# Attention, MLP and experts on one core: the decay of the keys as two rows of the score product

## Chip, core and metric

One core of a Trainium2 chip. The metric is the device time of the program in microseconds (us), the median of several runs; lower is better. In the profile, PE is the tensor engine's matmuls and PEld its weight loads, DVE is VectorE, ACT is ScalarE, POOL is GpSimd, and SP is the engine whose queue issues all the DMAs of this kernel.

## The reference

```python
def _attn_ref(q, k, v, s):                       # B, H, S, D = 2, 8, 576, 64
    scores = scale * np.matmul(q, k.transpose(0, 1, 3, 2))
    causal = np.triu(np.ones((S, S), dtype=bool), k=1)
    cum = np.cumsum(np.maximum(s, 0.0), axis=-1)
    bias = -(cum[:, :, :, None] - cum[:, :, None, :])
    scores = np.where(causal, -1000000000.0, scores + np.minimum(bias, 0.0))
    scores = scores - np.max(scores, axis=-1, keepdims=True)
    attn = np.exp(scores)
    attn = attn / (np.sum(attn, axis=-1, keepdims=True) + 1e-09)
    return np.matmul(attn, v)

x = attention output as (1152 tokens, 512)
h = x @ w_in;  x = np.maximum(0.01 * h, h) @ w_out                # 512 -> 2048 -> 512
out = sum over 4 experts e of p[:, e] * (np.maximum(x @ w1[e], 0) @ w2[e])   # 512 -> 1024 -> 512
```

Below the diagonal the bias is the key's decay sum less the query's. The query's part is the same for a whole row of the softmax and falls out, so the kernels add only the decay sum of the key.

## The kernel before

**Numbers.** Many matmuls use each operand as a pair of fp32r tiles: a high part (a cast on ACT) and the rest (a subtraction on POOL or DVE). The weights of the first MLP are 64-bit values in DRAM. `convert` (L91 to L106) makes fp32 of them, 16 pieces in all: two DMAs of 512 KB at L99 into one of two buffers `r64` (named r in the trace), one pass on ACT (L102) and four on DVE (L103 to L106). The piece is written back for later use (L115), and split by ACT (L140) and POOL (L141).

**Attention.** It is cut into 16 units of one batch, one pair of heads and a range of query tiles of 128: first 8 early units (tiles 0 and 1, keys 0 to 255), then 8 late ones (tiles 2 to 4, all 576 keys). `attention` runs the (tile, head) items of the units in a row, each in four steps with a lag between them: `scores`, `transposes`, `values`, `finish`. `load_pair` issues the loads of a unit when the unit before it begins (of the first two at the start).
- `cumulative` makes the decay sums of the 16 heads (L386), and writes them to DRAM (`cum_d`, L390).
- `load_pair` loads keys (`kr`, two heads on 128 partitions) and queries, and the tile `nck`: the decay sums of the unit's two heads on all 128 partitions, by a DMA that reads the same two rows 128 times (L446). Only the first unit gets it from four small matmuls and two copies on ACT (L442, L443). In early units the queries go to zero-padded tiles `qz` (L436), and the product is one fp32 matmul (L477). In late units queries and keys are split, `qs` (L425, L426) and `ks` (L430, L431), and the product is two matmuls (L480).
- `scores` writes the mask with an `affine_select` on POOL into 128 columns of `nck` (L473), once for each of the 80 items. Then the matmul, and on DVE L481, which adds `nck` to the scores, scales them into `z` and takes the row's minimum into `mn`. ACT does the exponential (L485).

**Order.** The early units run alone at first (with the first weights fetched after the second). The late units are woven into the first MLP's products over the first 512 tokens (`weave`, RATE = 5 attention steps to one of the MLP's); what is left of the attention runs by itself, then the rest. The order of instructions on each engine is set when the kernel is built, by a scheduler that simulates the program, within the data's order. All DMAs go through SP's queue in that order, and since their eight semaphores take turns, at most eight are on their way.

In the quoted order of SP's queue below, `r_...` are pieces of 64-bit weights, `vs` values, `w_f` the write-back.

## Time and profile before

| | us |
|---|---|
| median of 3 runs | 747.65 (745.64 to 748.36) |
| the profiled execution, its own time | 745.97 |
| its span in the trace | 744.2 |
| PE busy | 714.9 (96%) |
| DVE busy | 441.6 (59%) |
| POOL busy | 360.0 (48%) |
| ACT busy | 330.0 (44%) |

The three runs differ by 2.7 us. The span is divided as follows, by the first scores, the end of the early units and the end of the attention: to 62 us the early units with the first weights, to 185 us the late units among the first MLP's products with the conversion of the weights, to 221 us the rest of the attention, and then the remaining MLP and the experts. Times in the rows are microseconds unless marked ns. "Idle before" is the idle time of an engine just ahead of the instructions of a row, and behind it stand what ended it.

### The profile page before, as it was taken

How to read it: one execution, taken by the hardware profiler on the slowest of the kernel's cores; microseconds unless marked ns; L12 is line 12 of the kernel's file. 1: busy time of each engine (PE TensorE's matmuls, PEld its weight loads, DVE VectorE, ACT ScalarE, POOL GpSimd, SP SyncE). 2: the span in 40 equal slices, each digit the busy share in tenths (PEclk: the TensorE clock that was granted, in tenths of full speed). 3: DMA queues.
4: the chain of work that ended last, by engine and by line, in shares of the span. 5: the costliest groups of instructions: out<-in, count | busy, mean ns of one | idle time of the engine just before them, and what ended most of it. 6: DMA issues, size and time to landing. Idle time of an engine off the chain costs nothing.

```text
span 744.2 us, 11570 instructions
## 1 busy us (share of the span) xinstructions
PE 714.9 (96%) x4284; PEld 647.6 (87%) x4284; DVE 441.6 (59%) x919; ACT 330.0 (44%) x723; POOL 360.0 (48%) x326
## 2 busy tenths in 40 slices
PE   8888979997999989999999999999999999999997
PEld 7677868886988889999998988989889898898996
DVE  4788989959549472773674443644435444454452
ACT  5776957667765365563351232322313223142220
POOL 3487736556318658885436270542705427053200
PEclk9888999998999999999999999999999999999999
DMA  6997685854001222321011110201102011020002
GB/s 165 245 329 256 226 264 199 252 196 148 33 2 57 67 77 95 105 85 57 30 57 57 56 58 1 86 29 57 57 0 86 29 58 57 1 76 10 1 29 99
DMA packets 42792, 70.56 MB, mean 95 GB/s; under 512 B 4432, under 2 KB 25168, under 8 KB 42736
## 3 DMA queue, kind: packets, MB, share of 16 engines
q1 hardware_dynamic: 42736, 69.84, 29.3%
q8 instruction: 33, 0.54, 0.3%
q14 instruction: 23, 0.19, 0.1%
HBM read 59.04 MB, written 10.78 MB: 94 GB/s over the span
## 4 chain that ended last, share of the span: by engine, by line
PE 84%; DVE 7%; DMA 3%; issue 2%; ACT 2%; SPq 1%; POOL 1%; POOLq 0%; DVEq 0%; ACTq 0%
PE ps_d L188 38%; PE ps_u L188 34%; PE ps_o L503 5%; PE ps_sc L480 3%; PE ps_pt L494 3%; DMA nck<-cum_d 2%; DVE raw L105 1%; DVE z L481 1%; DVE raw L106 1%; PE ps_sc L477 1%; SPq L81 1%; DVE st L505 1%; DVE raw L103 1%; PE nothing L379 1%; DVE raw L104 0%
## 5 line engine op out<-in xcount | busy, mean ns | idle before, releaser
L188 PE MATMUL ps_u<-t,w 128*128 128x320 f32 (+1 forms) x1680 | 236.9, 299 | 2.4 <-DVE y L226 1.6
L188 PEld LDWEIGHTS ps_u<-t,w 128*128 128x128 f32 x1680 | 233.0, 189 | 6.3 <-DVE y L226 1.9
L188 PE MATMUL ps_d<-w,ht 128*128 128x512 f32 x864 | 202.9, 390 | 0.0
L188 PEld LDWEIGHTS ps_d<-w,ht 128*128 128x128 f32 x864 | 160.1, 188 | 31.7
L141 POOL TENSOR_TENSOR w<-raw,w 128x1024 fp32r<-128x1024 f32 x40 | 99.2, 2491 | 150.0 <-ACT w L140 149.8
L284 ACT ACTIVATE ht<-ps_u 128x320 fp32r<-128x320 f32 (+1 forms) x128 | 50.6, 411 | 131.9 <-DVE ps_u L261 114.2
L300 DVE SCALAR_TENSOR_TENSOR oacc<-ps_d,pn,oacc 128x512 f32<-128x512 f32 x63 | 47.3, 750 | 104.0 <-PE ps_d L188 104.0
L188 PE MATMUL ps_d<-ht,w 128*128 128x320 f32 (+1 forms) x576 | 107.2, 341 | 0.3 <-issue 0.3
L188 PEld LDWEIGHTS ps_d<-ht,w 128*128 128x128 f32 x576 | 92.9, 190 | 8.3 <-issue 0.5
L133 POOL TENSOR_TENSOR w<-raw,w 128x512 fp32r<-128x512 f32 (+1 forms) x48 | 49.5, 1053 | 75.8 <-ACT w L132 75.8
L140 ACT CAST w<-raw 128x1024 fp32r<-128x1024 f32 x40 | 41.7, 1050 | 81.4 <-PE ps_d L188 70.2
L473 POOL TENSOR_SCALAR_AFFINE_SELECT nck<-nck 128x128 f32<-128x128 f32 x80 | 38.0, 487 | 73.8 <-DVE mn L481 40.7
L503 PEld LDWEIGHTS ps_o<-vs,pv 128*128 128x128 f32 x480 | 67.2, 206 | 6.0 <-DVE xo L509 3.2
L261 DVE TENSOR_TENSOR ps_u<-ps_u,tmp 128x320 f32<-128x320 f32 (+1 forms) x120 | 55.9, 470 | 25.5 <-PE ps_u L188 23.6
L503 PE MATMUL ps_o<-vs,pv 128*128 128x64 f32 x480 | 68.8, 282 | 1.9 <-DVE xo L509 1.8
L285 DVE SCALAR_TENSOR_TENSOR ht<-ps_u,ht 128x320 fp32r<-128x320 f32 (+1 forms) x128 | 56.3, 452 | 22.7 <-ACT ht L284 21.3
L261 DVE TENSOR_TENSOR tmp<-ps_u,tmp 128x320 f32<-128x320 f32 (+1 forms) x80 | 36.8, 463 | 43.3 <-PE ps_u L188 41.4
L133 POOL TENSOR_TENSOR w<-sums,w 128x1024 fp32r<-128x1024 f32 x24 | 58.2, 2427 | 7.8 <-ACT w L132 7.8
L485 ACT ACTIVATE z<-z,mn 128x256 f32<-128x256 f32 (+4 forms) x80 | 48.5, 607 | 20.8 <-DVE mn L481 18.5
L481 DVE CUSTOM_DVE_ANT_0 z<-ps_sc,nck 128x256 f32<-128x256 f32 (+4 forms) x80 | 40.6, 511 | 21.2 <-POOL nck L473 8.6
L188 PE MATMUL ps_u<-x,w 128*128 128x512 f32 x192 | 50.6, 408 | 0.5 <-ACT x L527 0.5
L480 PE MATMUL ps_sc<-ks,qs 128*128 128x128 f32 (+3 forms) x128 | 37.9, 386 | 11.5 <-DVE mn L481 9.4
(82 smaller groups left out, 779.9 us busy)
## 6 DMA issues: line engine op xcount, KB each, us to landing
raw<-in_moe_w_dram SPq DMA_DIRECT2D x32, 512.0 KB, 3.5
r<-in_moe_w_in_dram SPq DMA_DIRECT2D x16, 512.0 KB, 5.6
w_f<-raw SPq DMA_DIRECT2D x16, 512.0 KB, 3.3
r<-in_moe_w_out_dram SPq DMA_DIRECT2D x16, 512.0 KB, 5.6
raw<-w_f SPq DMA_DIRECT2D x16, 512.0 KB, 3.2
nck<-cum_d SPq DMA_DIRECT2D x8, 576.0 KB, 4.7
qr<-in_q_dram SPq DMA_DIRECT2D x16, 160.0 KB, 4.9
kr<-in_k_dram SPq DMA_DIRECT2D x8, 288.0 KB, 5.7
```

The source lines that it names most:

```text
L133: nc.gpsimd.tensor_tensor(lo, of, f32(hi), ALU.subtract)
L140: nc.scalar.copy(w[:, 0], raw)
L141: nc.gpsimd.tensor_tensor(w[:, 1], raw, f32(w[:, 0]), ALU.subtract)
L188: nc.tensor.matmul(ps, a, b, start=(i == 0 and not onto), stop=(i == len(pairs) - 1), skip_group_check=onto)
L261: nc.vector.tensor_tensor(to, of, x, ALU.add)
L284: nc.scalar.activation(hi, of, AF.Relu)
L285: nc.vector.scalar_tensor_tensor(lo, of, 0.0, f32(hi), ALU.max, ALU.subtract)
L300: nc.vector.scalar_tensor_tensor(oacc[tt], ps, p, oacc[tt], ALU.mult, ALU.add)
L480: nc.tensor.matmul(ps, self.qz[:, l, j, own], self.kr[:, j, keys], start=(l == 0), stop=(l == 1))
L481: nc.vector.tensor_tensor_reduce(out=z[:, keys], in0=ps, in1=nck[:, j, keys], scale=-(D ** -0.5), scalar=3.0e38 if pc == 0 else mn[:, 0:1] ...
L485: nc.scalar.activation(z, z, AF.Exp, bias=mn[:, pc : pc + 1], scale=-1.0, accum_out=self.st[i][:, j : j + 1])
L503: nc.tensor.matmul(o[:, j], pv[:, kt], self.vs[:, kt, j], start=(kt == 0), stop=(kt == i))
```

## The change

The mask becomes one fixed tile `mask` (made once: a memset and one affine_select), of which DVE adds a slice. The decay sums are rounded to fp32r and a rest (`cum2`), and these two rows are partitions 64 and 65 of the key tile, loaded by two small DMAs per unit (L442: from SBUF for the first unit, from `cum_d` for the others). The query tiles hold ones in these rows. An early product then runs over 66 rows (D + 2). The keys of an early unit stand in a tile `ke` of three buffers, the two heads side by side on 64 partitions. In a late unit `ks` has the high part of the keys on partitions 0 to 63 and the rest on 64 to 127; a second tile `kd` has a copy of the high part, made by a DMA from SBUF to SBUF (L439), and the two decay rows. The tile `kr` has one buffer instead of two.

```diff
-    cum_d = dram.tile([BH, S], F32, name="cum_d")
+    cum_d = dram.tile([2, BH, S], F32, name="cum_d")
+    mask = ap.tile([P, S], F32, name="mask", bufs=1)
...
-        cum0 = r64p.tile([P, 2048], F32R, tag="r64", name="cum0")[:BH, : 2 * half[0]].rearrange("p (l k) -> p l k", l=2)
-        nc.scalar.copy(cum0[:, 0], cum[:, : half[0]])
-        nc.vector.tensor_tensor(cum0[:, 1], cum[:, : half[0]], f32(cum0[:, 0]), ALU.subtract)
-        nc.sync.dma_start(cum_d, cum)
+        cum2 = r64p.tile([P, 2048], F32R, tag="r64", name="cum2")[:BH, : 2 * S].rearrange("p (l k) -> p l k", l=2)
+        nc.scalar.copy(cum2[:, 0], cum)
+        nc.vector.tensor_tensor(cum2[:, 1], cum, f32(cum2[:, 0]), ALU.subtract)
+        nc.sync.dma_start(cum_d.rearrange("l h k -> h l k"), f32(cum2))
+        nc.gpsimd.memset(mask, 0.0)
+        nc.gpsimd.affine_select(mask[:, S - P :], mask[:, S - P :], [[-1, P]], ALU.is_ge, MASKED, 0, 1)
...
     def load_pair(n, b, hp, i0, i1):
...
-        kr = ap.tile([P, S], F32, tag="kr", name="kr")
-        nc.sync.dma_start(kr[:, :q1], k[b].rearrange("h d s -> (h d) s")[rows, :q1])
...
+        if i0 == 0:
+            kd = early.tile([P, 2, half[0]], F32, tag="ke", name="ke", bufs=3)
+            nc.sync.dma_start(kd[:D], k_of)
+            qs = q_e[n % 3]
+            nc.sync.dma_start(qs[:D], q[b, heads, :, q0:q1].rearrange("h d s -> d h s"))
+            ks = None
+        else:
...
             for j in range(2):
-                own, other = slice(j * D, (j + 1) * D), slice((1 - j) * D, (2 - j) * D)
-                nc.scalar.copy(ks[own, j], kr[own])
-                nc.gpsimd.tensor_tensor(ks[other, j], kr[own], f32(ks[own, j]), ALU.subtract)
-            kr = ks
-        else:
-            qz = q_pads[n % 2]
-            for j in range(2):
-                nc.sync.dma_start(qz[j * D : (j + 1) * D, j, : q1 - q0], q[b, 2 * hp + j, :, q0:q1])
-        nck = ap.tile([P, 2, S], F32, tag="nck", name="nck")
-        if n == 0:
-...
-        else:
-            src = cum_d[h : h + 2, 0:q1]
-            nc.sync.dma_start(nck[:, :, :q1], bass.AP(tensor=src.tensor, offset=src.offset, ap=[[0, P], [S, 2], [1, q1]]))
+                nc.sync.dma_start(qr[j * D : (j + 1) * D], q[b, heads, :, q0:q1].rearrange("h d s -> d h s"))
+            qs = q_s[n % 2]
+            nc.scalar.copy(qs[:, 0], qr)
+            nc.gpsimd.tensor_tensor(qs[:D, 1], qr[:D], f32(qs[:D, 0]), ALU.subtract)
+            kr = ap.tile([P, 2, S], F32, tag="kr", name="kr", bufs=1)[:D]
+            nc.sync.dma_start(kr, k_of)
+            ks = ap.tile([P, 2, S], F32R, tag="ks", name="ks")
+            nc.scalar.copy(ks[:D], kr)
+            nc.gpsimd.tensor_tensor(ks[D:], kr, f32(ks[:D]), ALU.subtract)
+            kd = ap.tile([P, 2, S], F32R, tag="kd", name="kd")
+            nc.sync.dma_start(f32(kd[:D]), f32(ks[:D]))
+        for l in range(2):
+            decay = f32(cum2[h : h + 2, l, :q1]) if n == 0 else cum_d[l, h : h + 2, :q1]
+            nc.sync.dma_start(f32(kd[D + l : D + l + 1]), decay)
...
         def scores(self, i, j):
...
-            nc.gpsimd.affine_select(nck[:, j, a:kw], nck[:, j, a:kw], [[-1, P]], ALU.is_ge, MASKED, 0, 1)
...
-                if len(self.qz.shape) == 3:
-                    nc.tensor.matmul(ps, self.qz[:, j, own], self.kr[:, keys], start=True, stop=True)
+                if self.ks is None:
+                    nc.tensor.matmul(ps, self.qs[:DK, j, own], self.kd[:DK, j, keys], start=True, stop=True)
                 else:
-                    for l in range(2):
-                        nc.tensor.matmul(ps, self.qz[:, l, j, own], self.kr[:, j, keys], start=(l == 0), stop=(l == 1))
+                    nc.tensor.matmul(ps, self.qs[:, 0, j, own], self.ks[:, j, keys], start=True, stop=False)
+                    nc.tensor.matmul(ps, self.qs[:DK, 1, j, own], self.kd[:DK, j, keys], start=False, stop=True)
                 nc.vector.tensor_tensor_reduce(
-                    out=z[:, keys], in0=ps, in1=nck[:, j, keys], scale=-(D ** -0.5),
+                    out=z[:, keys], in0=ps, in1=mask[:, S - kw + keys.start : S - kw + keys.stop], scale=-(D ** -0.5),
```

What the scheduler makes of it, at three places. POOL, from its instructions for the third early unit to the first piece of weights (L141 is the low part of a piece; behind each instruction stand the semaphores it waits for), before:

```order
L473 AFFINE_SELECT nck<-nck 128x128 [waits DMAHW0_49,Pool_49]
L473 AFFINE_SELECT nck<-nck 128x128
L473 AFFINE_SELECT nck<-nck 128x128 [waits DVE_49] x2
L473 AFFINE_SELECT nck<-nck 128x128 [waits DMAHW5_49,Pool_49]
L473 AFFINE_SELECT nck<-nck 128x128
L473 AFFINE_SELECT nck<-nck 128x128 [waits DVE_49] x2
L473 AFFINE_SELECT nck<-nck 128x128 [waits DMAHW3_49,Pool_49]
L473 AFFINE_SELECT nck<-nck 128x128
L473 AFFINE_SELECT nck<-nck 128x128 [waits DVE_49] x2
L473 AFFINE_SELECT nck<-nck 128x128 [waits DMAHW2_49,Pool_49]
L473 AFFINE_SELECT nck<-nck 128x128
L473 AFFINE_SELECT nck<-nck 128x128 [waits DVE_49]
```

and after, from the last of the memsets to the second late unit's queries:

```order
L410 MEMSET qe_142 2x512
L410 MEMSET qe_144 2x512
L410 MEMSET qe_146 2x512
L392 AFFINE_SELECT mask<-mask 128x128 [waits Pool_49]
L432 TENSOR_TENSOR qs<-qr,qs 64x640 [waits DMAHW2_49,Activation_49]
L437 TENSOR_TENSOR ks<-kr,ks 64x1152 [waits DMAHW1_49,Activation_49,Pool_49]
L141 TENSOR_TENSOR w<-raw,w 128x1024 [waits Activation_49,Pool_49]
L141 TENSOR_TENSOR w<-raw,w 128x1024 [waits Activation_49]
L432 TENSOR_TENSOR qs<-qr,qs 64x640 [waits DMAHW4_49,Activation_49]
```

The affine_selects between the pieces are gone; nothing of the early units is left on POOL, and its first work after the start is the first late unit's split and the weights. SP's queue from the third unit's decay sums to the fifth unit's and the next weights, before:

```order
L446 DMA nck<-cum_d 128x2x256 [waits DMAHW0_49,DVE_49,Activation_49]
L99 DMA r_395<-in_moe_w_in_dram 128x2x512 [waits DMAHW1_49]
L436 DMA qz_138<-in_q_dram 64x256 [waits DMAHW2_49,PE_49]
L417 DMA kr<-in_k_dram 128x256 [waits DMAHW3_49,PE_49]
L436 DMA qz_138<-in_q_dram 64x256 [waits DMAHW4_49]
L446 DMA nck<-cum_d 128x2x256 [waits DMAHW5_49,DVE_49]
L448 DMA vs<-in_v_dram 128x2x128 [waits DMAHW6_49,PE_49]
L436 DMA qz_135<-in_q_dram 64x256 [waits DMAHW7_49,PE_49]
L417 DMA kr<-in_k_dram 128x256 [waits DMAHW0_49,PE_49]
L436 DMA qz_135<-in_q_dram 64x256 [waits DMAHW1_49]
L99 DMA r_395<-in_moe_w_in_dram 128x2x512 [waits DMAHW2_49]
L446 DMA nck<-cum_d 128x2x256 [waits DMAHW3_49,DVE_49]
L99 DMA r_405<-in_moe_w_in_dram 128x2x512 [waits DMAHW4_49]
L99 DMA r_405<-in_moe_w_in_dram 128x2x512 [waits DMAHW5_49]
```

and after, from the fourth unit's keys on:

```order
L422 DMA ke<-in_k_dram 64x2x256 [waits DMAHW2_49,PE_49]
L424 DMA qe_142<-in_q_dram 64x2x256 [waits DMAHW3_49]
L442 DMA ke<-cum_d 1x2x256 [waits DMAHW4_49]
L442 DMA ke<-cum_d 1x2x256 [waits DMAHW5_49]
L99 DMA r_353<-in_moe_w_in_dram 128x2x512 [waits DMAHW6_49]
L99 DMA r_353<-in_moe_w_in_dram 128x2x512 [waits DMAHW7_49]
L99 DMA r_363<-in_moe_w_in_dram 128x2x512 [waits DMAHW0_49]
L99 DMA r_363<-in_moe_w_in_dram 128x2x512 [waits DMAHW1_49]
L429 DMA qr<-in_q_dram 64x2x320 [waits DMAHW2_49]
L422 DMA ke<-in_k_dram 64x2x256 [waits DMAHW3_49,PE_49]
```

The first four weight loads stand in a row, behind the fourth unit's loads and ahead of the fifth's. Before, one half of the first piece stood ahead of the fourth unit's loads, the other among the fifth's, and the second piece behind these. SP's queue around the loads of a late unit in the middle of the attention, before:

```order
L446 DMA nck<-cum_d 128x1152 [waits DMAHW5_49,DVE_49]
L115 DMA w_f_73<-raw 128x1024 [waits DMAHW6_49,DVE_49]
L450 DMA vs<-in_v_dram 64x128 [waits DMAHW7_49,PE_49]
L423 DMA qr<-in_q_dram 64x2x320 [waits DMAHW0_49,Pool_49]
L423 DMA qr<-in_q_dram 64x2x320 [waits DMAHW1_49]
L99 DMA r_1551<-in_moe_w_in_dram 128x2x512 [waits DMAHW2_49]
L99 DMA r_1551<-in_moe_w_in_dram 128x2x512 [waits DMAHW3_49]
L417 DMA kr<-in_k_dram 128x576 [waits DMAHW4_49,Pool_49]
```

and after:

```order
L442 DMA kd<-cum_d 1x1152 [waits DMAHW7_49,PE_49]
L442 DMA kd<-cum_d 1x1152 [waits DMAHW0_49]
L446 DMA vs<-in_v_dram 64x128 [waits DMAHW1_49,PE_49]
L439 DMA kd<-ks 64x1152 [waits DMAHW2_49,Activation_49]
L429 DMA qr<-in_q_dram 64x2x320 [waits DMAHW3_49,Pool_49]
L429 DMA qr<-in_q_dram 64x2x320 [waits DMAHW4_49]
L115 DMA w_f_73<-raw 128x1024 [waits DMAHW5_49,DVE_49]
L99 DMA r_1883<-in_moe_w_out_dram 128x1024 [waits DMAHW6_49]
L434 DMA kr<-in_k_dram 64x2x576 [waits DMAHW7_49,Pool_49]
L99 DMA r_1883<-in_moe_w_out_dram 128x1024 [waits DMAHW0_49]
```

Where the broadcast load stood are two one-row loads, and the copy kd<-ks, which waits for ACT, stands ahead of the next unit's qr, the write-back and the next weight piece.

## Rows read from the trace of the kernel before

**Rows 1.** Windows: us, busy us (instructions) by engine, clock, DMA share, GB/s
```profile
0.00:62.00 62.00, 50.65 (x262) 42.23 (x262) 44.88 (x143) 39.28 (x120) 33.60 (x56) 0.85 0.86 257
62.00:185.00 123.00, 113.24 (x667) 98.75 (x666) 107.48 (x194) 87.96 (x174) 76.91 (x61) 0.94 0.66 215
185.00:221.00 36.00, 34.98 (x288) 32.88 (x287) 17.36 (x70) 26.06 (x65) 8.10 (x16) 1.00 0.06 19
221.00:744.00 523.00, 516.03 (x3073) 473.75 (x3073) 271.91 (x514) 176.69 (x365) 241.37 (x194) 1.00 0.16 53
```

**Rows 2.** The same view for 8 to 62 us
```profile
8.00:62.00 54.00, 44.47 (x238) 37.37 (x238) 41.65 (x138) 36.76 (x115) 30.45 (x41) 0.83 0.93 281
```

**Rows 3.** Chain of waits in 0 to 62 us, shares by line
```profile
by line: DMA nck<-cum_d 25.6%; PE ps_sc L477 9.4%; PE ps_o L503 9.1%; issue 7.3%; PE nothing L379 6.1%; DVE z L481 5.7%; DVE raw L105 4.8%; PE ps_pt L494 4.6%; DVE raw L103 4.1%; DVE raw L106 3.7%; POOL nck L473 3.4%; DVE st L505 2.7%; PE p
```

**Rows 4.** Waits, 0 to 62 us: line waited for, us, times, longest
```profile
POOL nck L473 <- DMA nck<-cum_d: 13.7, 6, 3.8
DVE z L481 <- POOL nck L473: 8.6, 6, 2.5
ACT qs L425 <- DMA qr<-in_q_dram: 2.0, 1, 2.0
```

**Rows 5.** Waits of PE in 62 to 185 us
```profile
PE ps_sc L480 <- DVE mn L481: 9.4, 4, 4.8
```

**Rows 6.** Groups to 222 us: busy us, mean ns | idle before, releasers
```profile
L106 DVE SCALAR_TENSOR_TENSOR raw<-r,raw 128x1024 uint32<-128x1024 uint32 x16 | 27.1, 1694 | 0.0
L505 DVE TENSOR_SCALAR st<-st 128x2 f32<-128x2 f32 x40 | 20.3, 507 | 5.5 <-ACT z L485 5.1
L473 POOL TENSOR_SCALAR_AFFINE_SELECT nck<-nck 128x128 f32<-128x128 f32 x80 | 38.0, 487 | 73.8 <-DVE mn L481 40.7 <-DMA nck<-cum_d 25.4 <-ACT nck L443 4.1
L141 POOL TENSOR_TENSOR w<-raw,w 128x1024 fp32r<-128x1024 f32 x14 | 36.5, 2607 | 3.3 <-ACT w L140 3.0
L431 POOL TENSOR_TENSOR ks<-kr,ks 64x576 fp32r<-64x576 f32 x16 | 24.7, 1545 | 3.5 <-issue 2.3
L426 POOL TENSOR_TENSOR qs<-qr,qs 128x640 fp32r<-128x640 f32 x8 | 17.5, 2190 | 11.5 <-ACT qs L425 11.5
```

**Rows 7.** Lines: shortest/median/longest ns, first, last start (L106: 62 to 185 us)
```profile
L505 DVE TENSOR_SCALAR st<-st x40: 150/169/2367, 9.6 to 214.5; 128x2 f32<-128x2 f32 x40
L473 POOL TENSOR_SCALAR_AFFINE_SELECT nck<-nck x80: 288/295/1298, 7.5 to 211.2; 128x128 f32<-128x128 f32 x80
L106 DVE SCALAR_TENSOR_TENSOR raw<-r,raw x13: 1211/1225/3067, 61.0 to 179.7; 128x1024 uint32<-128x1024 uint32 x13
```

**Rows 8.** Timeline at 171.8 us: start, duration
```profile
171.75 2.39 POOL L141 TENSOR_TENSOR w<-raw,w 128x1024 fp32r<-128x1024 f32 x1 [0.89 <-ACT w L140]
171.86 2.31 DVE L505 TENSOR_SCALAR st<-st 128x2 f32<-128x2 f32 x1
```

**Rows 9.** Timeline, VectorE's first score step
```profile
7.87 0.42 DVE L481 CUSTOM_DVE_ANT_0 z<-ps_sc,nck 128x256 f32<-128x256 f32 x1 [2.38 <-POOL nck L473]
```

**Rows 10.** DMA issues to 222 us: KB each, median us from issue to landing
```profile
nck<-cum_d SPq DMA_DIRECT2D x8, 576.0 KB, 4.7
kr<-in_k_dram SPq DMA_DIRECT2D x8, 288.0 KB, 5.7
qr<-in_q_dram SPq DMA_DIRECT2D x16, 160.0 KB, 4.9
r<-in_moe_w_in_dram SPq DMA_DIRECT2D x16, 512.0 KB, 5.6
cum_d<-cum SPq DMA_DIRECT2D x1, 36.0 KB, 1.6
```

**Rows 11.** Timeline, the last unit's key cast and first score product
```profile
192.05 0.67 ACT L430 CAST ks<-kr 64x576 fp32r<-64x576 f32 x1
202.41 0.45 PE L480 MATMUL ps_sc<-ks,qs 128*128 128x448 f32 x1
```

**Rows 12.** Waits of the DMA queue to 222 us
```profile
SPq L446 <- DVE mn L481: 21.2, 7, 8.3
```

More of the change, by code (lines that the diff above doesn't have):

```diff
@@ L367, in attention_moe_moe2 @@
     BH = B * H
-    cum_d = dram.tile([BH, S], F32, name="cum_d")
-    cum0 = None
-    pick = const.tile([BH, 2], F32R, name="pick")
+    cum_d = dram.tile([2, BH, S], F32, name="cum_d")
+    cum2 = None
+    mask = ap.tile([P, S], F32, name="mask", bufs=1)
     def cumulative():
-        nonlocal cum0
+        nonlocal cum2
         idle = ap.tile([P, P], F32, tag="idle", name="idle", bufs=1)
@@ L380, in cumulative @@
         pos, cum = (r64p.tile([P, 2048], F32, tag="r64", name=n)[:BH] for n in ("pos", "cum"))
-        nc.scalar.copy(pick, ident[:BH, :2])
         spos, zero, cum = pos[:, :S], pos[:, S : 2 * S], cum[:, :S]
@@ L396, in attention_moe_moe2 @@
         nc.gpsimd.memset(x[: P - S % P, QT - 1], 0.0)
-    q_pads = []
+    DK = D + 2
+    q_s = [ap.tile([P, 2, 2, S // 2 + 32], F32R, tag=f"q{i}", name="qs", bufs=1) for i in range(2)]
+    q_e = []
     def pads(pool):
-        for i in range(2):
-            x = pool.tile([P, 2, half[0]], F32, name=f"qz{i}")
-            q_pads.append(x)
-            for j in range(2):
-                nc.gpsimd.memset(x[(1 - j) * D : (2 - j) * D, j], 0.0)
+        ones = pool.tile([P, 2, S // 2 + 32], F32, name="ones")
+        nc.gpsimd.memset(ones[D:DK], 1.0)
+        for i in range(3):
+            x = pool.tile([P, 2, half[0]], F32, name=f"qe{i}")
+            q_e.append(x)
+            nc.gpsimd.memset(x[D:DK], 1.0)
+        for x in q_s:
+            nc.scalar.copy(x[D:DK, 1], ones[D:DK])
@@ L437, in load_pair @@
-        nck = ap.tile([P, 2, S], F32, tag="nck", name="nck")
-        if n == 0:
-            for j in range(2):
-                ps = ps_t.tile([P, 512], F32, tag="pt", name="ps_nck")[:, :q1]
-                for l in range(2):
-                    nc.tensor.matmul(ps, pick[:, j : j + 1].to_broadcast([BH, P]), cum0[:, l, :q1], start=(l == 0), stop=(l == 1))
-                nc.scalar.copy(nck[:, j, :q1], ps)
-        else:
-            src = cum_d[h : h + 2, 0:q1]
-            nc.sync.dma_start(nck[:, :, :q1], bass.AP(tensor=src.tensor, offset=src.offset, ap=[[0, P], [S, 2], [1, q1]]))
+        rows, heads, h = slice(hp * P, (hp + 1) * P), slice(2 * hp, 2 * hp + 2), b * H + 2 * hp
@@ new lines, in load_pair @@
+        vs = v_s[n % 4]
+        k_of = k[b, heads, :, :q1].rearrange("h d s -> d h s")
+        if i0 == 0:
[5 more added lines that the diff above has]
+        else:
+            qr = ap.tile([P, 2, S // 2 + 32], F32, tag="qr", name="qr", bufs=1)
+            for j in range(2):
+                nc.sync.dma_start(qr[j * D : (j + 1) * D], q[b, heads, :, q0:q1].rearrange("h d s -> d h s"))
[9 more added lines that the diff above has]
+            nc.sync.dma_start(f32(kd[:D]), f32(ks[:D]))
@@ L450, in load_pair @@
             nc.sync.dma_start(vs[P - S % P :, QT - 1].rearrange("p h c -> p (h c)"), v[b, full * P :, rows])
-        return kr, qz, nck, vs
+        return ks, kd, qs, vs
     class Unit:
@@ L458, in __init__ @@
             self.of, self.items = (b, hp, i0, i1), [(i, j) for i in reversed(range(i0, i1)) for j in range(2)]
-            self.kr, self.qz, self.nck, self.vs = load_pair(n, b, hp, i0, i1)
+            self.ks, self.kd, self.qs, self.vs = load_pair(n, b, hp, i0, i1)
             self.z, self.pv, self.st = {}, {}, {}
@@ L463, in scores @@
         def scores(self, i, j):
-            i0, nck = self.of[2], self.nck
+            i0 = self.of[2]
             a, _, kw = tiles[i]
```

13 lines of the change are left out of this document (removed).

## The prediction

> **What bounds the kernel now.** I read the stretches first [rows 1]. From 221 us on the tensor engine (PE) is busy 516.03 of 523 us: that part can only start sooner. From 185 to 221 us, the end of the attention, PE is busy 34.98 of 36. What can be won lies before 185 us, where PE idles 123 - 113.24 = 9.8 us of the second stretch, and 54 - 44.47 = 9.5 us of 8 to 62 us [rows 2]. So the two stretches can give at most 19.3 us at the clock they have (the granted clock is 0.83 of full in rows 2, 0.94 in the second row of rows 1; I count nothing for a change of it).
>
> Next I looked at who holds PE there. In 0 to 62 us the chain of waits gives 25.6% of the stretch, 15.9 us, to the broadcast load nck<-cum_d [rows 3]. The table of waits shows the path: GpSimd's affine_select L473 waits 13.7 us for that load, and VectorE's L481, the step behind the score product, waits 8.6 us for GpSimd [rows 4]. From 62 us on the load has no such place: what PE's scores wait for is the step L481 before, 9.4 us in four waits, up to 4.8 each [rows 5]. VectorE is then busy 107.48 of 123 us, most of it weight conversion (L103 to L106), and some of its instructions last far longer than their work: L505, on 128x2 elements, has a median of 169 ns but a mean of 507, and L106 a median of 1225 and a mean of 1694 [rows 6, 7]. One such instruction shows why: L505 begins at 171.86 and ends at 174.17, while GpSimd's L141 runs from 171.75 to 174.14 [rows 8]. VectorE stands still until GpSimd is done.
>
> **The change, part by part**, against the profiled execution (745.97 us, span 744.2).
>
> *Broadcast load gone, 0 to 62 us.* VectorE's waits on GpSimd are 8.6 us [rows 4], of which 2.38 are the first unit's, which has no broadcast load [rows 9]; 6.2 are left. The chain's 15.9 us [rows 3] overlap work of PE on other items, and PE's idle time caps them at 9.5 [rows 2]. So between 6.2 and 9.5, or nothing if something else is late at once (a rival). I take -6.5, near the lower end, because VectorE is busy 44.88 and ScalarE 39.28 of the 62 us [rows 1]: when a score is no longer late for its keys' decay, it is soon late for these. The two decay rows of a unit's keys go the old load's way, a unit ahead, and wait for no GpSimd; I cost them at nothing. If that cover failed, each unit would wait about the 1.6 us of a small load [rows 10].
>
> *The start.* The first unit had its decay from a product and a copy. Now its score product itself waits for two rows moved from the scan's result by DMA. The nearest rows: the write of cum_d lands in 1.6 us [rows 10], and of the present wait 2.38 us end at the first L481 at 7.87 [rows 9]. Some 3 us (a longer cast and subtraction, an issue, a landing) take the place of some 2; the cost is 0.6 to 2, and I take +1.1.
>
> *The weight loads come earlier.* In the new order four loads of 512 KB stand in one run on the DMA queue ahead of the fifth unit's keys (order above). At the 281 GB/s of this stretch [rows 2] that is 2097 KB / 281 = 7.5 us of transfers. They run beside the third and fourth unit, whose loads are ahead of them. Nothing on the path, 2 us if that cover is too thin; in return conversion starts a unit or two earlier, which I count under the rivals.
>
> *Eighty affine_selects gone.* They are 38.0 us of GpSimd's 38.0 + 36.5 + 24.7 + 17.5 = 116.7 us before 222 us [rows 6]. VectorE's excess is 40 x (0.507 - 0.169) + 16 x (1.694 - 1.225) = 13.5 + 7.5 = 21 us [rows 6, 7]. By share of time the affine_selects would own a third of it, 7 us. But most of them last 295 ns [rows 7], so one can hold VectorE only briefly. Weighted with the mean duration as well (38.0 x 0.487 = 18.5 of 18.5 + 36.5 x 2.607 + 24.7 x 1.545 + 17.5 x 2.190 = 190), they own a tenth, 2.1 us. Midway is 4.5; not all of VectorE's time is PE's, so I take -2.5. The ends are 0 and the 9.4 us of rows 5.
>
> By the Trainium skill, "SBUF — State Buffer", section "SBUF: two separate sides", the port that VectorE and GpSimd share is locked for a whole instruction and the loser blocks fully. The pair of rows 8, ending within 0.03 us, agrees. By it the saving is that of the lock's length, and the long instructions stay: 2.1 rather than 7 us, so that the sum, were all of it PE's, would end at 737.0 by the one and at 732.1 by the other.
>
> *DMA traffic.* Seven early loads of 128x2x256 fp32, 256 KB, and eight late ones of 576 KB go [rows 10]; 288 KB per late unit come back as the copy kd<-ks. Of it some 7 x 0.262 + 0.590 = 2.4 MB lay before 62 us, 2.4 MB / 257 GB/s = 9.4 us of the queue's work in a stretch with a DMA share of 0.86 [rows 1]. On the path it counts only where an engine waits for another transfer: 2.0 us for qr is the large one [rows 4], and 3 us is my bound for all with the small ones. I take -1.5, between 0 and -3. Against it: two late rows (k, and q as before) are now on 64 partitions. qr moves 160 KB in 4.9 us to 64 partitions, kr 288 KB in 5.7 to 128 [rows 10]; a k tile on 64 may take up to 288 x 4.9 / 160 = 8.8 us. It is loaded a unit ahead, so nothing, and 3.1 us for a unit whose cover is too short.
>
> The Trainium skill, the same page, section "Door 1: The DMA port swizzle", says that 64 neighbouring partitions reach half of the ports. The 30.6 ns per KB of qr against 19.8 of kr agree in direction, though the sizes differ too. By it the freed 9.4 us would partly be eaten; with nothing left of them the sum is 1.5 higher.
>
> *Copy, casts, products.* One cast of 64x1152 replaces two of 64x576, the subtractions likewise, and the late product has the same columns: nothing. The copy kd<-ks waits for ScalarE's cast and stands at the head of the one DMA queue (order above). At the end of the attention there is room: in the last unit the second cast is issued at 192.05 and the first score at 202.41, about 10 us [rows 11], and PE is nearly full anyway [rows 1], so nothing is won or lost from 185 to 221. Before that the copy is a rival.
>
> Sum: -6.5 + 1.1 - 2.5 - 1.5 = -9.4, so 736.6 as the profiled run counts. That run is 1.7 us under the median (747.65), so I forecast **738 us**. Its own bounds: at best all of PE's idle time but the start, -19.3 + 0.6; at worst the lead is lost (below).
>
> **The rivals.**
> *No change.* The lead of the early units is given back. After 62 us PE is 92% and VectorE 87% busy [rows 1], and the 13 last conversions follow each other every (179.7 - 61.0) / 12 = 9.9 us [rows 7]; if that pace holds the products that need the weights, then an earlier attention only waits longer. Left is the 2.5 us of the affine_selects: 743.5, or 745.2 as a median. For it: the conversion begins early in both kernels. Against it: in the new order its loads begin earlier too.
> *Slower.* The copy kd<-ks waits at the head of SP's queue for a cast, with qr, a write-back and the next weight loads behind it. The broadcast load was held there too, 21.2 us in seven holds, up to 8.3 [rows 12], but it waited for scores already under way, and the copy waits for a cast of keys that must first land. A weight piece takes 5.6 us to land [rows 10] and is wanted every 9.9 us [rows 7], so a hold decides from 9.9 - 5.6 = 4.3 us on. Were it the 8.3 us of rows 12 in six late units, 6 x 4.0 = 24 us would be added, and VectorE's 2.5 would be lost in waiting: 745.97 - 6.5 + 1.1 - 1.5 + 24 = 763, or 765. Against it: the keys are loaded a unit ahead, and a hold of 3.0 us, the mean of rows 12, costs nothing.
> *Smaller gain.* VectorE's long instructions stay, since L141, L426 and L431 hold them as in rows 8, and the slower loads eat the DMA term: -6.5 + 1.1 = -5.4, so 740.6, or 742.2. (The lock of the Trainium skill's "SBUF — State Buffer", section "SBUF: two separate sides", would have it so: a short GpSimd step can hold VectorE only for its own length.)
> *Larger gain.* All of PE's idle time goes: -19.3 + 0.6 = -18.7, so 727.3, or 729. For it: the waits named are on one chain. Against it: PE also waits for casts and sums that nobody changes.
>
> **How the numbers follow.** The forecast has 0.44, no change 0.19, slower 0.13, the smaller gain 0.14, the larger 0.10. About 0.5% (3.7 us: 743.9 to 751.4) is what a measurement of this kernel can tell from no change. Faster by more is forecast, smaller and larger gain, 0.68; within it 0.19; slower 0.13. For 8 in 10 I leave out the slower case and the far part of the larger gain and reach a little past no change: 725 to 750.
>
> **What would show it.** In the profile of the changed kernel: no wait of VectorE's score step on GpSimd before 62 us, and the last early unit's transposed output some 6 us sooner; the first score step at about 9.0 us instead of 7.87; L505 nearer to 169 ns in the mean, though not at it; PE's wait on L481 in the late units shorter; the attention's end near 211 us instead of 221, and nothing but that shift behind it. I am wrong if SP's queue shows long holds at the copy, if ScalarE's first conversion step waits for weight loads, or if the early units end sooner and the attention does not.

## The result: 1.5% slower

The changed kernel takes 759.44 us (756.5 to 760.57, 4 runs) against 748.0 us (745.64 to 749.46): a ratio of 1.015, 95% interval 1.0111 to 1.0189. The forecast was 738 us, with 725 to 750 as its range. The profiled execution took 759.2 us, with a span of 757.4.

Where the time went is seen from two steps that end the stages: the cast of an early unit's transposed output (the first and last start of eight) and the copy of a late one's. Of the kernel before:

```profile
L524 ACT CAST x<-ps_x x8: 352/360/378, 17.5 to 73.2; 128x256 fp32r<-128x256 f32 x8
L527 ACT COPY x<-ps_x x8: 403/422/427, 106.4 to 221.3; 128x320 f32<-128x320 f32 x8
```

Of the changed kernel:

```profile
L519 ACT CAST x<-ps_x x8: 350/372/372, 25.2 to 85.0; 128x256 fp32r<-128x256 f32 x8
L522 ACT COPY x<-ps_x x8: 403/421/431, 111.4 to 232.8; 128x320 f32<-128x320 f32 x8
```

The first early output is 7.7 us late, the last, at 85 us, 11.8. (Before, the last early output came at 73.2 us, so the boundary of 62 us in [rows 1] lies ahead of the end of the early units.) Of the late ones, which run among and behind them, the first is 5.0 us late and the last 11.5: they stand better for a while and lose that again. Behind the attention no more than 1.7 of the 13.2 us is added by which the span grew. The stretches that answer to [rows 1], shifted by 12 us:

```profile
0.00:74.00 74.00, 58.67 (x230) 49.84 (x231) 51.69 (x139) 42.02 (x116) 22.97 (x24) 0.60 0.75 214
74.00:197.00 123.00, 117.31 (x709) 103.53 (x709) 97.24 (x204) 86.87 (x174) 48.77 (x20) 0.96 0.61 186
197.00:233.00 36.00, 34.26 (x272) 31.79 (x270) 16.78 (x63) 24.20 (x60) 4.17 (x3) 0.98 0.05 10
233.00:757.00 524.00, 516.39 (x3072) 474.03 (x3072) 271.83 (x514) 176.40 (x365) 241.16 (x194) 1.00 0.16 52
```

The columns are those of [rows 1]. The last is as before, and the two ahead of it hold 709 + 272 products where it had 667 + 288. In the first, 12 us longer, PE has 230 products where the kernel before had 262 in 62 us, and its granted clock is 0.60 instead of 0.85. Ten-microsecond windows show it better; of the kernel before, then of the changed one, each with a last row from the start to the end of the attention:

```profile
10.00:20.00 10.00, 9.18 (x59) 8.11 (x58) 4.80 (x29) 6.75 (x28) 2.80 (x10) 0.87 0.82 222
50.00:60.00 10.00, 6.82 (x39) 5.22 (x39) 9.23 (x20) 5.91 (x19) 8.25 (x8) 1.00 1.01 361
0.00:222.00 222.00, 199.36 (x1213) 174.15 (x1214) 170.32 (x407) 153.95 (x360) 119.07 (x133) 0.92 0.61 194
```

```profile
10.00:20.00 10.00, 10.00 (x40) 8.70 (x39) 5.08 (x28) 6.07 (x23) 0.00 (x0) 0.50 0.55 168
50.00:60.00 10.00, 8.98 (x39) 8.03 (x39) 8.99 (x21) 6.92 (x21) 2.36 (x1) 0.50 0.98 288
0.00:233.00 233.00, 210.24 (x1208) 185.15 (x1208) 165.71 (x406) 153.09 (x350) 75.92 (x47) 0.85 0.57 167
```

From 10 to 20 us PE is busy without a pause in the changed kernel, and yet it finishes 40 products where the kernel before finishes 59. The clock is at 0.50 of full, its lower level of 1.2 GHz, in each of the five windows from 10 to 60 us; in the kernel before it falls there too (0.66 to 1.00 in these windows), but comes back each time. The last rows sum it up: PE's idle time to the end of the attention is 222 - 199.4 = 22.6 us before and 233 - 210.2 = 22.8 after. **No idle time was won, and PE's busy time grew by 10.9 us for nearly the same products (1208 for 1213).** One form of product in 10 to 60 us (mean duration behind the busy time), before and after:

```profile
L477 PE MATMUL ps_sc<-kr,qz 128*128 128x256 f32 x28 | 12.0, 521 | 0.2
```

```profile
L472 PE MATMUL ps_sc<-ke,qe 66*128 66x256 f32 x27 | 14.8, 656 | 3.0 <-DVE mn L476 3.0
```

Here 128*128 is the part of the array that the product fills (rows, columns): 128 rows before, 66 after. The same 256 columns take 656 instead of 521 ns on average, where the 521 mixes stretches at both clocks, and the values' products, which nobody changed, 394 instead of 308.

Once more, from 190 to 200 us, the changed kernel's PE is busy all along at a low clock:

```profile
190.00:200.00 10.00, 10.00 (x50) 9.38 (x49) 3.41 (x16) 4.74 (x12) 0.10 (x1) 0.57 0.49 112
```

The start is later as well. PE's dummy products end at 4.53 us, then PE waits for the second decay row:

```profile
1.06 3.47 PE L380 MATMUL nothing<-idle 128*128 128x128 f32 x16 [1.06 <-DVE idle L377]
8.96 0.77 PE L472 MATMUL ps_sc<-ke,qe 66*128 66x256 f32 x1 [4.43 <-DMA ke<-cum]
10.32 0.42 DVE L476 CUSTOM_DVE_ANT_0 z<-ps_sc,mask 128x256 f32<-128x256 f32 x1 [4.11 <-PE ps_sc L472]
```

The first score step on VectorE begins at 10.32 instead of 7.87 us [rows 9].

### The profile page after: what moved, and what is told of

The parts are those of the page before. It is cut to its first block, busy times and chain, and to the rows that moved or that the text cites. A ratio compares the mean times of both kernels' runs of the same rounds, so it can differ in the third digit from the quotient of the medians.

```text
span 757.4 us, 11334 instructions
## 1 busy us (share of the span) xinstructions
PE 726.6 (96%) x4280; PEld 659.2 (87%) x4280; DVE 437.5 (58%) x919; ACT 329.5 (44%) x714; POOL 317.1 (42%) x240
## 4 chain that ended last, share of the span: by engine, by line
PE 75%; DVE 10%; DMA 4%; ACT 3%; issue 3%; POOL 2%; SPq 2%; ACTq 0%; POOLq 0%; DVEq 0%
PE ps_d L188 35%; PE ps_u L188 30%; PE ps_o L498 4%; PE ps_pt L489 2%; DVE raw L105 2%; DVE raw L106 2%; PE ps_sc L474 1%; PE ps_sc L475 1%; DMA qr<-in_q_dram 1%; DVE z L476 1%; DVE st L500 1%; DVE raw L103 1%; DMA r<-in_moe_w_out_dram 1%; POOL w L133 1%; DMA r<-in_moe_w_in_dram 1%
## 5 line engine op out<-in xcount | busy, mean ns | idle before, releaser
L141 POOL TENSOR_TENSOR w<-raw,w 128x1024 fp32r<-128x1024 f32 x40 | 97.6, 2453 | 205.2 <-ACT w L140 205.0
L498 PEld LDWEIGHTS ps_o<-vs,pv 128*128 128x128 f32 x480 | 73.4, 222 | 7.8 <-DVE xo L504 3.0
L498 PE MATMUL ps_o<-vs,pv 128*128 128x64 f32 x480 | 73.0, 296 | 4.1 <-DVE xo L504 2.3
L476 DVE CUSTOM_DVE_ANT_0 z<-ps_sc,mask 128x256 f32<-128x256 f32 (+4 forms) x80 | 40.7, 512 | 24.2 <-PE ps_pt L489 9.1
L489 PE MATMUL ps_pt<-ident,z 128*128 128x128 f32 x240 | 47.9, 306 | 2.5 <-ACT pv L490 1.0
L490 ACT COPY pv<-ps_pt 128x512 f32<-128x512 f32 (+3 forms) x96 | 39.2, 422 | 19.3 <-PE ps_pt L489 19.0
```

The lines of the kernel that those rows point to most:

```text
L141: nc.gpsimd.tensor_tensor(w[:, 1], raw, f32(w[:, 0]), ALU.subtract)
L476: nc.vector.tensor_tensor_reduce(out=z[:, keys], in0=ps, in1=mask[:, S - kw + keys.start : S - kw + keys.stop], scale=-(D ** -0.5), scalar ...
L489: nc.tensor.transpose(pt[:, (kt - k0) * P : (kt - k0 + 1) * P], z[:, tiles[kt][0] : tiles[kt][2]], ident)
L498: nc.tensor.matmul(o[:, j], pv[:, kt], self.vs[:, kt, j], start=(kt == 0), stop=(kt == i))
```

## The experiments

Three causes could be told from this: the rows of the early products, the gap ahead of the first score, or the new order of the weight loads. All ratios are against the kernel before, run on the same chip, with the 95% interval.

**The changed kernel again.** No edit.

> The changed kernel once more, for a second trace and more pairs of clock and time. Theory C (clock): the gap of 4.4 us in PE's work ahead of the first score (4.5 to 8.96 us) lets the granted clock fall to half, and it stays there to about 65 us; executions whose mean clock is near 0.99 should then be some 8 to 12 us shorter than those near 0.95. Theory W (weights and loads): the four weight loads in one run, and the loads behind them, set the pace of the first 85 us, and the clock costs nothing because PE would only wait; times then do not follow the clock (759 us at either).

Measured: 756.26 us, 1.0149 (1.0129 to 1.0169). Its time did not follow the mean clock (755.35 at 0.994, 756.03 at 0.954), which seems to speak against the clock. The products say otherwise:

```profile
10.00:20.00 10.00, 10.00 (x40) 8.71 (x39) 5.08 (x28) 6.07 (x23) 0.00 (x0) 1.00 0.56 175
L472 PE MATMUL ps_sc<-ke,qe 66*128 66x256 f32 x27 | 14.8, 655 | 3.0 <-DVE mn L476 3.0
```

This record says a clock of 1.00, and the products take 655 ns and come 40 to the window as where it says 0.50. So here the column is not to be trusted, and the duration of one form is. What follows rests on durations. The Trainium skill says the same in "TensorE: Matmul & The Clock Gate", section "Part 1: The HAM clock gate (the "warmup" mystery)": the clock's events in a trace can be unreliable. This pair of runs agrees.

**The gap.** 12 or 18 dummy products instead of 8:

```diff
-        for _ in range(8):
+        for _ in range(12):        # e1_warm18: range(18)
             nc.tensor.matmul(nothing[:, :P], idle, idle, start=True, stop=True)
```

> The changed kernel with 12 instead of 8 dummy products at the start, so that PE's gap ahead of the first score shrinks from 4.4 to some 2.7 us; the loads keep their order. Theory C: if the shorter gap keeps the clock, the first early output comes some 4 to 5 us sooner and the total is 747 to 752 us; if it does not, nothing changes. Theory W: 757 to 760 us whatever the clock shows.

> The changed kernel with 18 dummy products, which fill PE's gap ahead of the first score; the scheduler then also places the first four weight loads one unit later, behind the fifth unit's keys. Theory C: clock near full in the first 60 us, total 745 to 750 us. Theory W: the weights come later, but the early units' loads are not behind them; 752 to 757 us from the order alone, with or without the clock.

Measured: 758.11 us, 1.0171 (1.0141 to 1.020), and 1.0125 (1.0093 to 1.0156) for four executions of e1_warm18 from 753.38 to 764.16 us; two more took 765.1 and 770.37. With 18 the idle time ahead of the first score fell from 4.4 to 1.9 us, but the form 66x256 still took 645 ns. The gap alone is not the cause. Nor is the order of the weight loads: with 18 they were issued at 19.6 us, behind the fifth unit's keys, instead of at 15.2 ahead of them.

**The first unit's decay by products** onto the score product, instead of two rows by DMA:

```diff
+                if self.n == 0:
+                    nc.tensor.matmul(ps, self.qs[:D, j, own], self.kd[:D, j, keys], start=True, stop=False)
+                    for l in range(2):
+                        nc.tensor.matmul(ps, pick[:, j : j + 1].to_broadcast([BH, P]), cum2[:, l, keys], start=False, stop=(l == 1))
```

> The changed kernel, but the first unit gets its decay from two small products added onto the score product, instead of from two rows moved by DMA. Its first score step should be back near 7.9 us instead of 10.3, with PE's gap 2 to 3 us shorter. If the late start itself is the loss: 2 to 3 us less, 757 us. Theory C: the clock is kept as well, 746 to 751 us. Theory W: 757 us at most less the 2 us of the start.

Measured: 763.97 us, 1.0227 (1.0164 to 1.029), no faster than the changed kernel. The start did come sooner, and won nothing: the first score step on VectorE began at 7.56 us, a little ahead of the kernel before, the first early output at 20.5, but the last at 88.3. The early score product took 650 ns as before:

```profile
L525 ACT CAST x<-ps_x x8: 344/367/379, 20.5 to 88.3; 128x256 fp32r<-128x256 f32 x8
```

**The rows.** Early products of the changed kernel over 128 rows, the added ones zero; and those of the kernel before over 64:

```diff
+            y = pool.tile([P, 2, half[0]], F32, name=f"ke{i}")     # fixed tiles, used in turn
+            nc.gpsimd.memset(x[D:], 0.0)                           # x: the tile of qe
             nc.gpsimd.memset(x[D:DK], 1.0)
+            nc.gpsimd.memset(y[D:], 0.0)
-                    nc.tensor.matmul(ps, self.qs[:DK, j, own], self.kd[:DK, j, keys], start=True, stop=True)
+                    nc.tensor.matmul(ps, self.qs[:, j, own], self.kd[:, j, keys], start=True, stop=True)
```

```diff
-                    nc.tensor.matmul(ps, self.qz[:, j, own], self.kr[:, keys], start=True, stop=True)
+                    nc.tensor.matmul(ps, self.qz[j * D : (j + 1) * D, j, own], self.kr[j * D : (j + 1) * D, keys], start=True, stop=True)
```

> The changed kernel with its early score products over 128 instead of 66 rows: the 62 added rows of both operands are zero, so the columns and the result stay. Theory R (rows): in the early units PE is busy all of the time from 10 to 25 us and still has the half clock, which the kernel before, with 128 rows, leaves after a few us; products over 66 rows do not bring the clock back. Then the clock is near full for most of 10 to 60 us, the mean of a product 66x256 falls from 0.65 to some 0.52 us and the total is 742 to 749 us. Theory G (the gap at the start, which the dummy products did not fill well, or the weights' order): 753 to 760 us.

> The kernel before with one edit: an early score product runs over the 64 rows of its own head instead of over 128 rows of which 64 meet zeros. Same columns, same result, same loads. Theory R: the clock stays at half for most of the first 60 us and the total rises by 5 to 11 us, to 750 to 757. Theories G and W (weights): 743 to 747 us.

Measured: e5 750.37 us, 1.0058 (1.0034 to 1.0082); e6 755.75 us, 1.0131 (1.0103 to 1.0158). The forms of e5 and of e6 in 10 to 60 us:

```profile
L476 PE MATMUL ps_sc<-ke,qe 128*128 128x256 f32 x32 | 12.6, 490 | 6.2 <-DMA ke<-cum 6.2
```

```profile
L477 PE MATMUL ps_sc<-kr,qz 64*128 64x256 f32 x24 | 14.6, 710 | 3.5 <-DMA kr<-in_k_dram 2.0 <-DVE mn L481 1.4
```

490 ns over 128 rows, 710 over 64. The kernel before lost 10 us by this one edit. But the scheduler weighs rows, so both edits also changed the order of the instructions; e13 and e14, below, take that out.

**The parts.** Only the early units changed, or only the late ones; the other half is the code of the kernel before. Against the changed kernel, cut to the lines that matter:

```diff
 # e3: late units as before
+            nc.sync.dma_start(kd, bass.AP(tensor=src.tensor, offset=src.offset, ap=[[0, P], [S, 2], [1, q1]]))
+                nc.gpsimd.affine_select(self.kd[:, j, a:kw], self.kd[:, j, a:kw], [[-1, P]], ALU.is_ge, MASKED, 0, 1)
-                    nc.tensor.matmul(ps, self.qs[:DK, 1, j, own], self.kd[:DK, j, keys], start=False, stop=True)
 # e4: early units as before
+                nc.sync.dma_start(nck[:, :, :q1], bass.AP(tensor=src.tensor, offset=src.offset, ap=[[0, P], [S, 2], [1, q1]]))
-                    nc.tensor.matmul(ps, self.qs[:DK, j, own], self.kd[:DK, j, keys], start=True, stop=True)
```

> Only the early units are changed; the late ones get the broadcast load and their affine_selects back. Theory R or G, both of which put the loss into the early units: 753 to 760 us. If the late units' copy and loads cost the time: 738 to 746 us.

> Only the late units are changed; the early ones are those of the kernel before. Theory R or G: 741 to 747 us, with the clock of the kernel before in the first 60 us. If the late units' copy and loads cost the time: 753 us and more.

Measured: e3 747.72 us, 1.0019 (1.0003 to 1.0036), with 647 ns for the form 66x256; e4 749.32 us, 1.0057 (1.003 to 1.0083), with 483 ns for 128x256. Theory R, which gave e3 753 to 760, missed: the early products are slow, and the kernel is within 0.4% of the one before. The outputs of e3:

```profile
L521 ACT CAST x<-ps_x x8: 345/351/375, 24.2 to 88.3; 128x256 fp32r<-128x256 f32 x8
L524 ACT COPY x<-ps_x x8: 401/410/425, 111.8 to 223.5; 128x320 f32<-128x320 f32 x8
```

Its early units end at 88.3 us, later even than in the changed kernel, and its late ones only 2.2 us later than before: behind the early units most of the delay was made up. And e4 missed too: the kernel with the late change alone is 4 us slower, without the early units' lasting low clock. Nor do the parts add up: 1.0019 x 1.0057 is 1.0076, half of the loss.

**One order, two numbers of rows.** The scheduler's simulation of time left out of e5, so that e13 and e14 have the same order on all five engines; the products' line is all that e14 changes in e13:

```diff
-    with _tile.TileContext(nc, schedule_with_timeline_sim=True) as tc:
+    with _tile.TileContext(nc, schedule_with_timeline_sim=False) as tc:     # e13 and e14
 # e14 alone
-                    nc.tensor.matmul(ps, self.qs[:, j, own], self.kd[:, j, keys], start=True, stop=True)
+                    nc.tensor.matmul(ps, self.qs[:66, j, own], self.kd[:66, j, keys], start=True, stop=True)
```

> e5_rows128 (all units changed, early products over 128 rows), but with the scheduler's simulation of time left out, so that the order no longer depends on the rows; it is the mate of e14_plain66, whose instructions stand in the same order on every engine. Its own time is open, 755 to 800 us, since the order is another; the early products 128x256 should last about 0.5 us.

> e13_plain128 with the early products over 66 rows and nothing else, in the same order on every engine. Theory R: products of about 0.65 us in the first 60 us, and the total 5 to 12 us above e13's. If the 10 us between the kernel before and e6_before64, and the 9 us between the changed kernel and e5_rows128, came from the order that the scheduler made anew and not from the rows: within 2 us of e13.

Measured: e13 767.83 us (765.97 to 770.18), e14 780.3 us (777.88 to 783.78): 12.5 us for the rows. The windows to 60 us and to the same count of 1256 products, and the form, of e13 and then of e14:

```profile
0.00:60.00 60.00, 46.67 (x265) 40.09 (x266) 33.77 (x132) 34.87 (x113) 15.97 (x26) 0.94 0.46 134
0.00:239.00 239.00, 208.89 (x1256) 180.28 (x1256) 166.56 (x407) 154.65 (x356) 78.85 (x50) 0.95 0.49 143
L476 PE MATMUL ps_sc<-ke,qe 128*128 128x256 f32 x32 | 11.9, 480 | 8.4 <-DMA ke<-cum_d 8.2 <-DVE mn L480 0.2
```

```profile
0.00:60.00 60.00, 51.50 (x209) 45.77 (x209) 30.26 (x115) 30.37 (x96) 11.77 (x24) 0.57 0.39 119
0.00:252.00 252.00, 223.54 (x1256) 194.52 (x1256) 169.47 (x408) 155.46 (x356) 78.80 (x50) 0.86 0.46 136
L476 PE MATMUL ps_sc<-ke,qe 66*128 66x256 f32 x30 | 15.6, 642 | 7.4 <-DMA ke<-cum 7.4
```

For the same 1256 products in the same order PE is busy 223.5 instead of 208.9 us, while its idle time is 239 - 208.9 = 30.1 and 252 - 223.5 = 28.5. The 0.94 of e13 is too high: its record has 1.00 from the start to 20 us, where the form 128x256 took 596 ns from 10 to 20 us. So e13 fell to the lower level as well, but it had left it by 20 us. From 20 to 30 us, e13 and then e14, and the last two early products of each, in e13 between 50 and 60 us and in e14 between 60 and 70:

```profile
20.00:30.00 10.00, 9.30 (x65) 7.83 (x65) 9.03 (x40) 8.59 (x31) 0.00 (x0) 1.00 0.40 122
L476 PE MATMUL ps_sc<-ke,qe 128*128 128x256 f32 x2 | 0.7, 407 | 0.0
```

```profile
20.00:30.00 10.00, 10.00 (x44) 9.34 (x45) 5.90 (x26) 5.68 (x22) 0.00 (x0) 0.50 0.36 107
L476 PE MATMUL ps_sc<-ke,qe 66*128 66x256 f32 x2 | 0.7, 407 | 0.0
```

At the higher level the product takes 407 ns over 66 rows as over 128: fewer rows do not make it slower in itself, the clock does. That settles the rows: in this order, with the early products over 66 rows PE stays at its lower clock nearly to the end of the early units, even where it never pauses.

**What the early change is worth with full rows.** e7 is e3 with 128 rows; e15 asks besides for the first weights one unit earlier; e10 has besides the first unit's decay by products, as e2:

```diff
 # e7
+            nc.gpsimd.memset(x[D:], 1.0)
+            (nc.gpsimd if i else nc.vector).memset(y[D:], 0.0)
-                    nc.tensor.matmul(ps, self.qs[:DK, j, own], self.kd[:DK, j, keys], start=True, stop=True)
+                    nc.tensor.matmul(ps, self.qs[:, j, own], self.kd[:, j, keys], start=True, stop=True)
 # e15
-                if done == 2:
+                if done == 1:
```

> Early units changed as in e3_early_only, and their products over 128 rows (64 rows of ones in the queries, zeros under them in the keys, set once); the late units are those of the kernel before. Theory R: e3 lost to the half clock what it won by dropping the broadcast load, so this one wins it: 736 to 742 us, the last early output some 5 us ahead of e3's, with products 128x256 at about 0.5 us. If the broadcast load was worth nothing in the first place: 744 to 748 us as e3.

> e7_early128 (early units changed, 128 rows, late units as before) with the first weights asked for after the first early unit instead of the second; in the queue's order their four loads then stand one unit earlier. In e7 the third weight piece began its conversion at 52.4 us, in the kernel before at 41.8. If the weights' pace holds the lead of the early units (the rival 'no change'): 740 to 743 us. If it does not: 745 to 747, or anything up to 755 from the new order alone, as e10 showed.

> e7_early128 (early units changed, products over 128 rows, late units as before), and the first unit's decay added by two small products instead of by two rows moved by DMA. In e7's trace PE's first score waits 4.3 us for those rows. Theory S (the start is on the path of everything behind it): 2 to 3 us less than e7's 745.8, that is 742.5 to 744, which is ahead of the kernel before. If the start is made up for later by the weights' pace: 745 to 746.

Measured: e7 745.76 us, 0.999 (0.997 to 1.001); e15 746.88 us, 0.999 (0.9964 to 1.0017); e10 753.79 us, 1.0097 (1.0068 to 1.0127). The early units of e7, then what PE waited for behind the attention:

```profile
L524 ACT CAST x<-ps_x x8: 350/352/373, 18.6 to 68.2; 128x256 fp32r<-128x256 f32 x8
L527 ACT COPY x<-ps_x x8: 404/418/428, 100.9 to 217.6; 128x320 f32<-128x320 f32 x8
PE ps_d L188 <- POOL w L141: 1.1, 1, 1.1
```

Its last early output is 5 us sooner than before, the last late one 3.7 us, and its profiled execution (744.6 us) only 1.4 us shorter than that of the kernel before. Part of the lead is seen to go behind the attention, where PE now waits 1.1 us for a piece of weights; where the rest goes is not shown. Whether the weights' pace holds the lead is not shown either: e15 began its first conversion at 21.7 instead of 25.3 us, but the third at 51.6, where e7 has 52.4. Nor is the cause of e10's loss of 8 us: its edit does bring the first score product to 5.4 us, and it comes with another order.

So the price of 66 rows depends on what stands around them: 12.5 us at equal order; by the ratios, and with another order as well, 1.3% or 10 us in the kernel before (e6), 0.9% or 7 in the changed one (e0 against e5), 0.3% or 2 without the late change (e3 against e7).

**The late units' 4 us.** Four edits of e5, each with its own order: the long subtraction in two; the second late product over 128 rows, the added ones zero; the copy by a second cast instead of the DMA; two buffers for `kr`:

```diff
 # e8
-            nc.gpsimd.tensor_tensor(ks[D:], kr, f32(ks[:D]), ALU.subtract)
+            for j in range(2):
+                nc.gpsimd.tensor_tensor(ks[D:, j], kr[:, j], f32(ks[:D, j]), ALU.subtract)
 # e9
-                    nc.tensor.matmul(ps, self.qs[:DK, 1, j, own], self.kd[:DK, j, keys], start=False, stop=True)
+                    nc.tensor.matmul(ps, self.qs[:, 1, j, own], self.kd[:, j, keys], start=False, stop=True)
 # e11
-            nc.sync.dma_start(f32(kd[:D]), f32(ks[:D]))
+            nc.scalar.copy(kd[:D], kr)
 # e12
-            kr = ap.tile([P, 2, S], F32, tag="kr", name="kr", bufs=1)[:D]
+            kr = ap.tile([P, 2, S], F32, tag="kr", name="kr", bufs=2)[:D]
```

> e5_rows128 with one edit: GpSimd's subtraction of the late keys, 64x1152 in one piece of 2.6 us, is made in two of 64x576, one for each head, as the kernel before has it. Theory L (the long piece holds VectorE until it ends; in the trace of the changed kernel L500 stood from 203.12 to 205.12 us beside a piece from 202.48 to 205.10, and PE waited): 1 to 4 us less than e5's 750.4, that is 746 to 749, and the step from the fifth last to the fourth last late output back from 11.9 to some 10.5 us. Otherwise 750 as e5.

> e5_rows128 with the second late score product over 128 instead of 66 rows, the 62 added rows zero. Theory R also for the late units (a fifth of PE's work there runs over 66 rows): fewer stretches at half clock between 60 and 200 us and 2 to 5 us less than e5's 750.4, that is 745 to 748. If the late units' loss is not the clock's: 750 to 752 us, with the longer memsets at the start.

> e5_rows128 with one edit: the second copy of the late keys' high part is made by a second cast on ScalarE (some 1.1 us each) instead of by the DMA from SBUF to SBUF that waits on SP's queue for the first cast. If that DMA on the queue is the late units' loss of some 4 us: 746 to 748. If not: 750 to 752, with ScalarE's 9 us more work.

> e5_rows128 with two buffers for the late keys as loaded (kr) instead of one, as the kernel before has it, so that the next unit's load needs not wait for GpSimd's subtraction. If late loads of keys are the late units' loss: 746 to 748. If not: 750 as e5.

Measured: e8 750.12 us, 1.0052 (1.0024 to 1.008); e9 749.18 us, 1.0029 (1.0003 to 1.0056); e11 762.69 us, 1.0222 (1.0189 to 1.0256); e12 754.05 us, 1.0106 (1.0058 to 1.0154). None is shown to bring back the 4 us. The subtraction does hold VectorE in the changed kernel:

```profile
202.48 2.62 POOL L437 TENSOR_TENSOR ks<-kr,ks 64x1152 fp32r<-64x1152 f32 x1
203.12 2.00 DVE L500 TENSOR_SCALAR st<-st 128x2 f32<-128x2 f32 x1 [1.77 <-ACT z L480]
```

L500, 169 ns of work, stands from 203.12 to 205.12 beside a GpSimd step that ends at 205.10, as in [rows 8]; but cutting that step in two did not shorten the kernel. As the changed kernel from 190 to 200 us, e12 ran at a low clock late in the attention, for 20 us without a pause:

```profile
180.00:200.00 20.00, 20.00 (x87) 19.07 (x87) 5.90 (x27) 10.93 (x25) 4.17 (x2) 0.50 0.29 84
```

Late products over 66 rows are not needed for that. In e9, which has no product over 66 rows, PE was as slow from 192 to 202 us. The durations agree: the values' products took 405 ns in the stretch of e12 and 407 in this one, but 268 in e9 from 180 to 190 us:

```profile
192.00:202.00 10.00, 9.96 (x42) 9.28 (x43) 3.44 (x15) 3.99 (x9) 0.00 (x0) 0.50 0.00 0
```

By the ratios e9 is 0.3% faster than e5, with intervals that overlap. What the late units' loss is made of stays open. With e5, e8, e9 and e12 from 749 to 754 us for nearly the same work, it may be the order alone; no pair of runs at one order tests that.

## Why the prediction was wrong, step by step

- **What bounded the kernel** was read rightly as far as it went: the loss too lies in the attention. But idle time of PE was taken for all that could move. PE's busy time moved, by 10.9 us, more than the whole gain that was forecast.
- **The step that failed** is the one on products ("the late product has the same columns: nothing"), together with "the granted clock is 0.83 of full ... I count nothing for a change of it". The early product had the same columns and 66 instead of 128 rows, and got no term at all. What the runs showed in its place: products over 66 rows left PE at its lower clock, where a product of this form takes 642 instead of 407 ns (e14), and that cost 12.5 us at equal order (e13, e14) and 7 to 10 in the two kernels themselves (e5, e6, with another order as well). With full rows the change came to 750.4 us, a ratio of 1.0058. So the rows account for 0.9 of the 1.5%; the rest is still a loss and not the forecast gain, and its cause stays open.
- **Broadcast load, -6.5.** The waits did go: no score step waits for GpSimd before 74 us. With the late units as before and full rows the early units end 5 us sooner (e7), near the term; as time it is worth 0.1%, within its interval nothing. For this part of the change that is the outcome of the rival "no change", which had 0.19; its mechanism, the weights' pace, is not shown (e15).
- **The start, +1.1 (0.6 to 2).** It was 10.32 - 7.87 = 2.45 us, above the upper end. In front of the product itself the queue issued the first decay row at 5.94 us, then the write of `cum_d`, and the second row at 7.21; the product began at 8.96.
- **Affine_selects, -2.5.** On VectorE the saving was there. The groups that answer to [rows 6]:

```profile
L106 DVE SCALAR_TENSOR_TENSOR raw<-r,raw 128x1024 uint32<-128x1024 uint32 x16 | 26.6, 1664 | 0.1
L500 DVE TENSOR_SCALAR st<-st 128x2 f32<-128x2 f32 x40 | 18.0, 451 | 12.7 <-ACT z L480 12.4
```

  With the medians of 169 and 1218 ns the excess is 40 x (0.451 - 0.169) + 16 x (1.664 - 1.218) = 18.4 us against 21: 2.6 us less, near the 2.1 that weighting by duration gave and far from 7. Most of the excess is left, as it would be if GpSimd's long steps made it, which the rival "smaller gain" held. In the total nothing of the saving is seen.
- **The slower rival** had the right sign and the wrong mechanism. The queue's holds at the copy kd<-ks:

```profile
SPq L439 <- ACT pv L490: 3.4, 3, 1.9
SPq L439 <- ACT ks L436: 1.7, 2, 1.0
SPq L439 <- ACT z L480: 0.4, 1, 0.4
SPq L442 <- PE ps_sc L475: 16.0, 5, 9.0
```

  The copy's holds are 5.5 us in all, the longest 1.9: under the 4.3 from which it was to decide. e11, without the copy, was no faster, though with another order and more work on ACT. Longer holds are at the decay rows that took the broadcast load's place (the last line): 16.0 us in five, up to 9.0, much as the old load's [rows 12]. What they cost is not shown.
- **DMA, -1.5.** 66.5 instead of 70.56 MB moved. The trace of the changed kernel has no landing times, so the loads to 64 partitions could not be priced, and no run singles this term out.

## What to carry to other kernels

A product with the same columns takes the same time at the same clock, but it need not leave the clock where it was: before fewer rows are counted as free, look at what PE's clock does in that stretch, and price the stretch at the lower level too (here 407 ns for one form at the higher level and 642 to 656 in stretches at the lower). Zero rows that look like waste may hold the clock up, and can be put back for a memset. Where a scheduler orders the work, compare edits at one order, or take their differences of a few microseconds for the order's.
